# Loading a global filter's inputs in fp32 on one queue, with conversions on GpSimd, VectorE and ScalarE

## The chip, the cores and the metric

The kernel runs on one core of one Trainium2 chip. The metric is device time in microseconds for one launch; several runs are taken and their median is given. A profile of one execution comes with each kernel. The engines are named as the profile does: PE (TensorE matmul), PEld (its weight loads), DVE (VectorE), ACT (ScalarE), POOL (GpSimd) and SP (SyncE, which here only issues transfers; SPq is its instruction queue).

## The reference

Eight batches of 3,200 positions with 256 channels. A circular convolution along the sequence with a learned filter per channel, done in the frequency domain, and then a gated layer: a causal depthwise convolution of five taps gives a gate, which multiplies a projection, and a second projection follows. Inputs and output are fp32.

```python
X = np.fft.rfft(x, axis=1)                      # x: (8, 3200, 256)
Y = X * (filt_r + 1j * filt_i)[None]            # filt: (1601, 256)
x = np.fft.irfft(Y, n=3200, axis=1)
gate_pre = sum(conv_w[k] * xp[:, k:k + S, :] for k in range(5))   # causal, xp is x with 4 zeros ahead
gate = 1 / (1 + np.exp(-gate_pre))
out = (gate * (x @ w_val)) @ w_out
```

## The kernel before

The transform of length 3,200 = 128 x 25 is done in two stages of matmuls with tables of sines and cosines that the kernel makes itself at the start. For each batch the work is cut into seven chunks (NCH), and seven helper functions each do one stage of one chunk:

- `s1`: 128-point transform of a chunk of `xt` with the table `cf_t` into PSUM, DVE copies it to bf16 (`so`), SP stores it to a scratch tensor in DRAM (`dscr`).
- `load_t`: loads `tt` back from `dscr` in another layout, so that the 25-point transforms lie along the partitions. This relayout needs all seven stores of the batch.
- `s2`: the 25-point transforms (tables `wc_t`, `ws_t`, `wsn_t`), ACT copies PSUM to `xs`, and DVE multiplies by the filter in three operations, `za`, `zb` and `z` (with `fr_t`, `fm_t`, which hold the filter).
- `inva`: the inverse 25-point transforms (`vc_t`, `vs_t`, `vsn_t`), ACT copies to `u`, SP stores to a second scratch tensor, `escr`.
- `load_v`: loads `vt` back from `escr` in the first layout; again all of a batch's stores must have landed.
- `invb`: the inverse 128-point transform (`ci_t`), which leaves the result `yt` channel-major; ACT copies it.
- `conv`, `val`, `outp`: the five taps as diagonal matmuls (`dg_t`) with a sigmoid on ACT (`gt`); the projection, multiplied on DVE (`gv`); the output projection, copied to `o` by DVE or ACT in turn and stored by SP.

A loop over sub-steps G starts, in each, one chunk of each stage, with a lag between stages: `s2` runs 9 sub-steps after `s1`, `inva` 10, `invb` 19, `conv` 21, `val` 22, `outp` 23. All seven `load_t` of a batch are called at once after its last `s1`, and all seven `load_v` after its last `inva`. Four PSUM tiles are shared by all stages in turn, so that a stage's matmuls wait until the tile of an earlier stage has been copied out.

The order on each engine is made by the framework's scheduler from the program's order and its estimates; the helpers' order in the loop is a preference, not a rule. Each engine executes its own list in order. SP carries all transfers but three kinds: x (line 86), the filter (lines 216 to 225) and the two projection weights are issued by POOL, in a form of transfer that converts fp32 to bf16 on the way. Ten `xt` buffers hold x, so POOL issues a load as soon as an `s1` has freed one.

Before the loop the tables are made: DVE reduces angles with `floormod` (seven operations, lines 103 to 113), ACT takes sines, and `expand` (line 171) spreads each table in thirteen small operations. The `s1` of batch 0 belongs to the loop's first sub-steps.

Of the kernel before, what the change touches and what calls it, by code (L numbers as in the profile page):

```python
# [15 lines left out]
PI = math.pi  # L16
# [19 lines left out]
def kernel(  # L36
# [31 lines left out]
    b_npi = cpool.tile([128, 1], FP32, name="b_npi")  # L68
# [3 lines left out]
    xpool = ctx.enter_context(tc.tile_pool(name="xin", bufs=10))  # L72
    spool = ctx.enter_context(tc.tile_pool(name="s1o", bufs=4))
    tpool = ctx.enter_context(tc.tile_pool(name="s2i", bufs=8))

    def psum():
        return pp.tile([128, 1024], FP32, name="ps", tag="ps")

# [3 lines left out]
    def load_x(b, j):  # L82
        p0, np_ = PCH[j]
        xt = xpool.tile([128, 4, D], BF16, name="xt")
        src = x[b].rearrange("(a r) d -> a r d", r=R)[:, p0:p0 + np_, :]
        nc.gpsimd.dma_start(out=xt[:, 0:np_, :], in_=src)  # L86
        xts[(b, j)] = xt

    for j in range(NCH):
        load_x(0, j)  # L90


    with tc.tile_pool(name="gen", bufs=1) as g1, \
         tc.tile_pool(name="gen2", bufs=2) as g2, \
         tc.tile_pool(name="genf", bufs=1) as gf:

        def floormod(src_ap, divisor):
            shp = list(src_ap.shape)
            divi = g2.tile(shp, I32, name=f"fm_i{shp[1]}")
            bak = g2.tile(shp, FP32, name=f"fm_b{shp[1]}")  # L100
            q = g2.tile(shp, FP32, name=f"fm_q{shp[1]}")
            cm = g2.tile(shp, FP32, name=f"fm_c{shp[1]}")
            nc.vector.tensor_scalar(divi[...], src_ap, 1.0 / float(divisor), None,
                                    op0=ALU.mult)
            nc.vector.tensor_copy(bak[...], divi[...])
            nc.vector.scalar_tensor_tensor(q[...], bak[...], -float(divisor), src_ap,
                                           op0=ALU.mult, op1=ALU.add)
            nc.vector.tensor_scalar(cm[...], q[...], float(divisor) - 0.5, None,
                                    op0=ALU.is_ge)
            nc.vector.scalar_tensor_tensor(q[...], cm[...], -float(divisor), q[...],  # L110
                                           op0=ALU.mult, op1=ALU.add)
            nc.vector.tensor_scalar(cm[...], q[...], -0.5, None, op0=ALU.is_lt)
            nc.vector.scalar_tensor_tensor(q[...], cm[...], float(divisor), q[...],
                                           op0=ALU.mult, op1=ALU.add)
            return q

        def iota(shape, pattern, base, cm, name):
            t = g1.tile(shape, FP32, name=name)
            nc.gpsimd.iota(t[...], pattern=pattern, base=base, channel_multiplier=cm,
                           allow_small_or_imprecise_dtypes=True)  # L120
            return t

        nc.vector.memset(b_npi[:, :], -PI)
        pcol = iota([128, 1], [[0, 1]], 0, 1, "pcol")


        kc = iota([128, NG, 2, GL], [[5, NG], [0, 2], [1, GL]], 1, 0, "kc")
        nc.vector.memset(kc[:, NG - 1, 0, GL - 1:GL], 0.0)
        pr = g1.tile([128, NG, 2, GL], FP32, name="pr")
        nc.vector.tensor_scalar(pr[...], kc[...], pcol[:, 0:1], None, op0=ALU.mult)  # L130
        nc.vector.tensor_scalar(pr[:, :, 0, :], pr[:, :, 0, :], 0.75 * L, None,
                                op0=ALU.add)
        q = floormod(pr[...].rearrange("p g c l -> p (g c l)"), L)
        nc.scalar.activation(cf_t[:, :], q[...], AF.Sin, bias=b_npi[:, 0:1],
                             scale=2.0 * PI / L)

        ident = g1.tile([128, 128], FP32, name="ident")
        nc.vector.memset(ident[:, :], 1.0)
        nc.gpsimd.affine_select(out=ident[:, :], in_=ident[:, :], pattern=[[1, 128]],
                                compare_op=ALU.is_equal, fill=0.0, base=0,  # L140
                                channel_multiplier=-1)
        idh = g1.tile([128, 128], FP16, name="idh")
        nc.vector.tensor_copy(idh[:, :], ident[:, :])


        rq = floormod(pcol[...], R)
        lp = g1.tile([128, 1], FP32, name="lp")
        nc.vector.tensor_tensor(lp[...], pcol[...], rq[...], op=ALU.subtract)
        nc.vector.tensor_scalar(lp[...], lp[...], 1.0 / R, None, op0=ALU.mult)
        rp = g1.tile([128, 1], FP32, name="rp")  # L150
        nc.vector.tensor_copy(rp[...], rq[...])
        lw = g1.tile([128, 1], FP32, name="lw")
        nc.vector.tensor_scalar(lw[...], pcol[...], 4.0 * R - 0.5, None, op0=ALU.is_ge)
        nc.vector.tensor_scalar(lw[...], lw[...], -65.0, None, op0=ALU.mult)


        mk = g1.tile([128, GL, R], FP16, name="mk")
        mkf = g1.tile([128, GL, R], FP32, name="mkf")
        nc.vector.memset(mkf[...], 1.0)
        nc.gpsimd.affine_select(out=mkf[...], in_=mkf[...], pattern=[[-R, GL], [0, R]],  # L160
                                compare_op=ALU.is_ge, fill=0.0, base=0,
                                channel_multiplier=1)
        nc.gpsimd.affine_select(out=mkf[...], in_=mkf[...], pattern=[[R, GL], [0, R]],
                                compare_op=ALU.is_ge, fill=0.0, base=R - 1,
                                channel_multiplier=-1)
        nc.vector.tensor_copy(mk[...], mkf[...])

        def expand(dst, src):
            nc.gpsimd.memset(dst[:, :, P2:128], 0.0)
            for g in range(NG):  # L170
                nc.vector.tensor_tensor(
                    dst[:, g, 0:P2].rearrange("p (l r) -> p l r", l=GL),
                    src[:, g, :].unsqueeze(1).to_broadcast((128, GL, R)),
                    mk[...], op=ALU.mult)

        def negate(dst, src):
            nc.vector.tensor_scalar(dst[...], src[...], -1.0, None, op0=ALU.mult)

        def sincos(prod, dc, ds, dsn):
            qs = floormod(prod[...].rearrange("p g r -> p (g r)"), N)  # L180
            sn = g2.tile([128, NG, R], FP16, name="sn")
            nc.scalar.activation(sn[...].rearrange("p g r -> p (g r)"), qs[...],
                                 AF.Sin, bias=b_npi[:, 0:1], scale=2.0 * PI / N)
            pc = g2.tile([128, NG, R], FP32, name="pc")
            nc.vector.tensor_scalar(pc[...], prod[...], 0.75 * N, None, op0=ALU.add)
            qc = floormod(pc[...].rearrange("p g r -> p (g r)"), N)
            cs = g2.tile([128, NG, R], FP16, name="cs")
            nc.scalar.activation(cs[...].rearrange("p g r -> p (g r)"), qc[...],
                                 AF.Sin, bias=b_npi[:, 0:1], scale=2.0 * PI / N)
            expand(dc, cs)  # L190
            expand(dsn, sn)
            negate(ds, dsn)

        HK = R // 2 + 1
        kv = g1.tile([128, NG, R], FP32, name="kv")
        nc.gpsimd.iota(kv[:, :, 0:HK], pattern=[[5, NG], [L, HK]], base=1,
                       channel_multiplier=0, allow_small_or_imprecise_dtypes=True)
        nc.gpsimd.iota(kv[:, :, HK:R], pattern=[[5, NG], [-L, R - HK]],
                       base=1 + L * (R - 1), channel_multiplier=0,
                       allow_small_or_imprecise_dtypes=True)  # L200
        nc.vector.tensor_scalar(kv[...], kv[...], lp[:, 0:1], None, op0=ALU.add)
        nc.vector.tensor_scalar(kv[:, NG - 1, :], kv[:, NG - 1, :], lw[:, 0:1], None,
                                op0=ALU.add)
        nc.vector.tensor_scalar(kv[...], kv[...], rp[:, 0:1], None, op0=ALU.mult)
        sincos(kv, wc_t, ws_t, wsn_t)


        fi_t = gf.tile([128, NG, D], BF16, name="fi_t")

        def fsrc(f, row, ap):  # L210
            return bass.AP(tensor=f.tensor, offset=f.offset + row * D, ap=ap + [[1, D]])

        for f, dst in ((filt_r, fr_t), (filt_i, fi_t)):
            for l in range(GL):
                ng = NG if l < GL - 1 else NG - 1
# [187 lines left out]
    def invb(b, j):  # L403
# [15 lines left out]
        if j == 0:  # L419
            nc.gpsimd.memset(y[:, :, 0:H, 0:1], 0.0)  # L420
            for dh in range(2):
                nc.gpsimd.tensor_copy(y[:, dh, 0:H, 1:L], y[:, dh, R:R + H, 0:L - 1])
# [68 lines left out]
    for G in range(total):  # L491
        c = at(G, -NCH)
        if c is not None:
            load_x(*c)
# [57 lines left out]
```

## Time and profile before

| | us |
|---|---|
| median of 3 runs (lowest, highest) | 386.45 (383.33, 387.43) |
| profiled execution | 387.95 |
| its span | 385.9 |
| PE busy, share | 312.3, 81% |
| DVE busy, share | 284.9, 74% |
| ACT busy, share | 229.1, 59% |
| POOL busy, share | 64.2, 17% |

The profile counts the time from the first to the last instruction as the span; the launch lies around it. Matmuls are pipelined and their ends are modelled, so a PE that is shown busy can still be waiting a little. The transfers moved 94.5 MB: 79.0 MB on the queue that SP feeds and 15.0 MB on the one that POOL feeds, counted in the bytes that are written. The mean clock of TensorE was 0.966 of full speed.

### The profile page before, as it was taken

The numbers are of one execution on the slowest core, as the hardware profiler recorded it, in microseconds if no ns is written. First come the engines' busy times: TensorE is split into PE (matmuls) and PEld (weight loads), VectorE is DVE, ScalarE is ACT, GpSimd is POOL, SyncE is SP. The second block draws the span as 40 slices with busy tenths as digits, with TensorE's granted clock in tenths as the row PEclk, the third lists the DMA queues.
The fourth block names the chain that finished last, engine by engine and source line by source line (L and its number), as shares of the span: only waits on it lengthen the run. The fifth ranks groups of instructions, "written<-read, shape, count | busy, mean of one in ns | idle before, by whom it ended". The sixth has DMA issues, their size and how long they took to land.

```text
span 385.9 us, 8019 instructions
## 1 busy us (share of the span) xinstructions
PE 312.3 (81%) x3089; PEld 206.9 (54%) x3089; DVE 284.9 (74%) x462; ACT 229.1 (59%) x255; POOL 64.2 (17%) x131
## 2 busy tenths in 40 slices
PE   0230477475899999999997999899999999999992
PEld 0100145253656756766675666566676677666661
DVE  4999958553858887888787789678977677765554
ACT  1100235334976777677765776677677878867660
POOL 8797211112110211021102011100010001001000
PEclk9999998766989999999999999999999999999998
DMA  7999999999999999999999999989595968449343
GB/s 124 144 162 190 216 257 251 231 250 280 179 250 249 311 286 273 263 282 332 274 301 303 286 269 298 285 299 319 201 351 170 304 223 299 136 142 323 141 191 152
DMA packets 94118, 94.53 MB, mean 245 GB/s; under 512 B 10102, under 2 KB 74624, under 8 KB 94080
## 3 DMA queue, kind: packets, MB, share of 16 engines
q1 hardware_dynamic: 80064, 78.98, 62.5%
q0 software_dynamic: 14016, 15.04, 28.1%
q8 instruction: 24, 0.39, 0.4%
q14 instruction: 14, 0.11, 0.1%
HBM read 56.59 MB, written 52.43 MB: 282 GB/s over the span
## 4 chain that ended last, share of the span: by engine, by line
PE 44%; DVE 20%; DMA 19%; SPq 8%; issue 4%; ACT 2%; POOL 1%; DVEq 0%; ACTq 0%; POOLq 0%
PE ps L431 12%; PE ps L448 7%; DMA escr<-u 6%; PE ps L465 6%; DVE so L310 6%; DMA vt<-escr 5%; SPq L326 5%; PE ps L413 5%; DMA dscr<-so 4%; PE ps L376 3%; DVE gv L453 3%; DMA tt<-dscr 3%; PE ps L378 3%; PE ps L307 3%; DVE za L354 2%
## 5 line engine op out<-in xcount | busy, mean ns | idle before, releaser
L415 ACT ACTIVATE yt<-ps 128x1024 bf16<-128x1024 f32 (+1 forms) x56 | 52.1, 931 | 44.3 <-PE ps L413 44.2
L453 DVE TENSOR_TENSOR gv<-ps,gt 128x1024 bf16<-128x1024 f32 (+1 forms) x56 | 61.9, 1104 | 18.7 <-PE ps L448 13.7
L310 DVE CAST so<-ps 128x1024 bf16<-128x1024 f32 (+1 forms) x56 | 61.5, 1103 | 19.0 <-PE ps L307 15.9
L354 DVE TENSOR_TENSOR za<-xs,fr_t 125x1024 bf16<-125x1024 bf16 (+1 forms) x56 | 37.3, 665 | 50.5 <-ACT xs L349 50.3
L381 ACT ACTIVATE u<-ps 125x1024 bf16<-125x1024 f32 (+1 forms) x56 | 53.9, 963 | 24.4 <-PE ps L378 21.6
L431 PE MATMUL ps<-yt,dg_t 64*64 64x512 bf16 (+1 forms) x1120 | 65.7, 361 | 0.8
L349 ACT ACTIVATE xs<-ps 125x1024 bf16<-125x1024 f32 (+1 forms) x56 | 54.0, 965 | 19.6 <-PE ps L346 18.4
L436 ACT ACTIVATE gt<-ps 128x1024 bf16<-128x1024 f32 (+1 forms) x56 | 52.4, 935 | 9.1 <-PE ps L431 5.9
L86 POOL DMA_DIRECT2D xt<-in_x_dram x56 | 30.2, 569 | 153.0 <-PE ps L307 146.5
L307 PE MATMUL ps<-xt,cf_t 128*128 128x512 bf16 x112 | 36.9, 421 | 22.4 <-DVE so L310 11.4
L465 PE MATMUL ps<-wo_t,gv 128*128 128x256 bf16 x400 | 52.8, 273 | 0.9 <-DVE gv L453 0.9
L448 PE MATMUL ps<-yt,wv_t 128*128 128x512 bf16 (+1 forms) x224 | 52.6, 357 | 0.0
L465 PEld LDWEIGHTS <-gv 128*128 128x128 bf16 x400 | 39.1, 98 | 14.9 <-DVE gv L453 1.2
L413 PE MATMUL ps<-ci_t,vt 128*128 128x128 f16 x400 | 31.9, 221 | 13.3 <-DMA vt<-escr 9.6
L431 PEld LDWEIGHTS <-dg_t 64*64 64x64 bf16 x1120 | 30.1, 106 | 23.2 <-issue 10.1
L340 PE MATMUL ps<-tt,wc_t 125*128 125x256 bf16 x104 | 30.1, 289 | 12.9 <-DMA tt<-dscr 10.6
L470 DVE COPY o<-ps 128x1024 f32<-128x1024 f32 (+1 forms) x32 | 36.7, 1148 | 1.1 <-PE ps L465 1.1
L360 DVE TENSOR_TENSOR z<-za,zb 125x1024 bf16<-125x1024 bf16 (+1 forms) x56 | 36.4, 650 | 1.3
L413 PEld LDWEIGHTS <-vt 128*128 128x128 bf16 x400 | 27.0, 98 | 17.9 <-DMA vt<-escr 10.7
L358 DVE TENSOR_TENSOR zb<-xs,fm_t 125x1024 bf16<-125x1024 bf16 (+1 forms) x56 | 36.2, 646 | 0.0
L376 PE MATMUL ps<-z,vc_t 125*128 125x256 bf16 x104 | 30.0, 289 | 6.9 <-DVE z L360 6.9
L307 PEld LDWEIGHTS <-cf_t 128*128 128x128 f16 x112 | 9.2, 108 | 41.7 <-issue 28.2
(109 smaller groups left out, 386.6 us busy)
## 6 DMA issues: line engine op xcount, KB each, us to landing
out_dram<-o SPq DMA_DIRECT2D x32, 512.0 KB
tt<-dscr SPq DMA_DIRECT2D x48, 256.0 KB
escr<-u SPq DMA_DIRECT2D x48, 224.0 KB
out_dram<-o SPq DMA_DIRECT2D x24, 384.0 KB
xt<-in_x_dram POOLq DMA_DIRECT2D x32, 256.0 KB, 6.5
dscr<-so SPq DMA_DIRECT2D x32, 256.0 KB
vt<-escr SPq DMA_DIRECT2D x32, 256.0 KB
xt<-in_x_dram POOLq DMA_DIRECT2D x24, 192.0 KB, 5.7
```

The lines of the kernel that those rows point to most:

```text
L307: nc.tensor.matmul(ps[:, a * D:e * D], lhsT=cf_t[:, 0:128], rhs=xt[:, a:e, :], start=True, stop=True)
L310: nc.vector.tensor_copy(so[:, 0:np_, :].rearrange("p a d -> p (a d)"), ps[:, 0:np_ * D])
L349: nc.scalar.activation(xs[0:P2, 0:ng, :, :].rearrange("p g c d -> p (g c d)"), ps[0:P2, 0:ng * 512], AF.Copy)
L354: nc.vector.tensor_tensor(za[0:P2, 0:ng], xs[0:P2, 0:ng], fr_t[0:P2, g0:g0 + ng, :].unsqueeze(2).to_broadcast((P2, ng, 2, D)), op=ALU.mult)
L381: nc.scalar.activation(u[0:P2, 0:2 * ng, :].rearrange("p q d -> p (q d)"), ps[0:P2, 0:ng * 512], AF.Copy)
L413: nc.tensor.matmul(ps[:, o:o + L], lhsT=v[:, a, 128 * dh:128 * dh + 128], rhs=ci_t[:, :], start=True, stop=True)
L415: nc.scalar.activation(y[:, :, H + p0:H + p0 + np_, :].rearrange("p h a n -> p h (a n)"), ps[:, :].rearrange("p (h n) -> p h n", h=2)[:, : ...
L431: nc.tensor.matmul(ps[64 * dh:64 * dh + 64, 512 * r:512 * r + np_ * L], lhsT=dg_t[rows, dh, k, :], rhs=y[rows, dh, p0 + k:p0 + k + np_, :] ...
L436: nc.scalar.activation(g[:, :, 0:np_ * L], ps[:, :].rearrange("p (h n) -> p h n", h=2)[:, :, 0:np_ * L], AF.Sigmoid)
L448: nc.tensor.matmul(ps[:, 512 * eh:512 * eh + np_ * L], lhsT=wv_t[:, dh, 128 * eh:128 * eh + 128], rhs=y[:, dh, H + p0:H + p0 + np_, :], st ...
L453: nc.vector.tensor_tensor(gv[:, :, 0:np_ * L], ps[:, :].rearrange("p (h n) -> p h n", h=2)[:, :, 0:np_ * L], g[:, :, 0:np_ * L], op=ALU.mult)
L465: nc.tensor.matmul(ps[:, D * a:D * a + D], lhsT=gv[:, eh, L * a:L * a + L], rhs=wo_t[:, eh, :], start=(eh == 0), stop=(eh == 1))
```

## The change

- x is loaded in fp32 by SP into six new buffers (`xf`), and POOL converts each chunk to bf16 (`cast_x`) into four `xt` buffers; before, POOL issued converting loads into ten.
- The filter is loaded in fp32 by SP, in pieces between the stores of batch 0's `s1`; DVE converts the real part (`fr_t`), ACT scales and converts the imaginary part (`fm_t`), which DVE did before.
- SP's list is exactly the program's order (`manual_schedule`). A sub-step's order is `invb`, `s2`, `conv`, `cast_x`, `s1`, `inva`, `load_x`, `load_t`, `load_v`, `val`, `outp`, with one `load_t` and one `load_v` in each sub-step. The loads of `tt` of batch 0 and of x of batch 1 alternate before the loop.
- Lags: `s2` 10, `inva` 11, `invb` 21, `conv` 23, `val` 24, `outp` 25. `s1` of batch 0 stands before the making of the other tables, and ACT copies its chunks 1, 3 and 5.
- Angles are reduced by adding and subtracting a large constant (three operations), `expand` is one operation per table, negation and `dg_t` go from DVE to ACT, and the shift of `yt` by one (before two operations on POOL) is one on DVE.
- Buffers: `za` and `zb` two instead of three, `o` three instead of four.

```diff
-    xpool = ctx.enter_context(tc.tile_pool(name="xin", bufs=10))
+    xpool = ctx.enter_context(tc.tile_pool(name="xin", bufs=4))
+    fpool = ctx.enter_context(tc.tile_pool(name="xf", bufs=6))
...
+    ctx.enter_context(tc.manual_schedule(engines={E.SP}))
...
     def load_x(b, j):
         p0, np_ = PCH[j]
+        xf = fpool.tile([128, 4, D], FP32, name="xf")
+        src = x[b].rearrange("(a r) d -> a r d", r=R)[:, p0:p0 + np_, :]
+        nc.sync.dma_start(out=xf[:, 0:np_, :], in_=src)
+        xts[(b, j)] = xf
+
+    def cast_x(b, j):
+        np_ = PCH[j][1]
+        xf = xts[(b, j)]
         xt = xpool.tile([128, 4, D], BF16, name="xt")
-        src = x[b].rearrange("(a r) d -> a r d", r=R)[:, p0:p0 + np_, :]
-        nc.gpsimd.dma_start(out=xt[:, 0:np_, :], in_=src)
+        nc.gpsimd.tensor_copy(xt[:, 0:np_, :], xf[:, 0:np_, :])
         xts[(b, j)] = xt
...
+        if b == 0 and j % 2 == 1:
+            st[("Sact", j)] = nc.scalar.activation(sov, ps[:, 0:np_ * D], AF.Copy)
+        else:
+            nc.vector.tensor_copy(sov, ps[:, 0:np_ * D])
...
+        def sine(dst, t):
+            r = g2.tile(list(t.shape), FP32, name=f"sr{t.shape[1]}")
+            nc.vector.tensor_scalar(r[...], t, MAGIC, None, op0=ALU.add)
+            nc.vector.tensor_scalar(r[...], r[...], -MAGIC, None, op0=ALU.add)
+            nc.vector.tensor_tensor(r[...], t, r[...], op=ALU.subtract)
+            nc.scalar.activation(dst, r[...], AF.Sin, scale=2.0 * PI * (1.0 - 2e-7))
...
+        for j in range(NCH):
+            s1(0, j)
+            if 1 <= j <= GL:
+                load_f(j - 1)
...
-        def expand(dst, src):
+        def expand(eng, dst, src):
             nc.gpsimd.memset(dst[:, :, P2:128], 0.0)
-            for g in range(NG):
-                nc.vector.tensor_tensor(
-                    dst[:, g, 0:P2].rearrange("p (l r) -> p l r", l=GL),
-                    src[:, g, :].unsqueeze(1).to_broadcast((128, GL, R)),
-                    mk[...], op=ALU.mult)
+            return eng.tensor_tensor(
+                dst[:, :, 0:P2].rearrange("p g (l r) -> p g l r", l=GL),
+                src[...].unsqueeze(2).to_broadcast((128, NG, GL, R)),
+                mk[...].unsqueeze(1).to_broadcast((128, NG, GL, R)), op=ALU.mult)
...
+        for j in range(NCH):
+            load_t(0, j)
+            load_x(1, j)
...
+        with tc.issue_after(vs_ins.ins):
+            nc.vector.tensor_copy(fr_t[0:P2, :, :], ff[0:P2, 0])
+        nc.scalar.activation(fm_t[0:P2, :, 0, :], ff[0:P2, 1], AF.Copy,
+                             scale=sgn[0:P2, 0:1])
+        nc.scalar.activation(fm_t[0:P2, :, 1, :], ff[0:P2, 1], AF.Copy,
+                             scale=sg[0:P2, 0:1])
...
         if j == 0:
-            nc.gpsimd.memset(y[:, :, 0:H, 0:1], 0.0)
-            for dh in range(2):
-                nc.gpsimd.tensor_copy(y[:, dh, 0:H, 1:L], y[:, dh, R:R + H, 0:L - 1])
+            nc.vector.memset(y[:, :, 0:H, 0:1], 0.0)
+            nc.vector.tensor_copy(y[:, :, 0:H, 1:L], y[:, :, R:R + H, 0:L - 1])
...
-    LAG_S2 = 9
-    LAG_IB = LAG_S2 + 10
+    LAG_S2 = 10
+    LAG_IB = LAG_S2 + 11
...
+    steps = [
+        (invb, LAG_IB, 0), (s2, LAG_S2, 0), (conv, LAG_IB + 2, 0), (cast_x, -2, 1),
+        (s1, 0, 1), (inva, LAG_S2 + 1, 0), (load_x, -NCH, 2), (load_t, NCH, 1),
+        (load_v, LAG_S2 + 1 + NCH, 0), (val, LAG_IB + 3, 0), (outp, LAG_IB + 4, 0),
+    ]
     for G in range(total):
...
+        for stage, lag, first in steps:
+            c = at(G, lag, first)
+            if c is not None:
+                stage(*c)
```

`load_f(l)` issues four transfers (eight for the last l) of twelve or thirteen partitions each. `at(G, lag, first)` gives the batch and chunk that a stage handles in sub-step G, and nothing for batches below `first`.

## The prediction

> **What bounds the kernel now.** I read the time in stages first. The span is 385.9 us, the profiled run 387.95 us, so 2.05 us lie around the span; the median of the three runs, 386.45, is 0.4% below that run. Cut at the first stage-2 matmul (45.0 us), at the first `invb` (92.7) and at the 35th `invb` (280.1), the windows view answers (columns: stretch, its length, busy us of PE, PEld, DVE, ACT and POOL with counts, TensorE clock, DMA share, GB/s):
>
> ```profile
> 0.00:45.00 45.00, 8.33 (x19) 2.13 (x19) 38.35 (x157) 3.96 (x6) 34.13 (x70) 1.00 1.09 164
> 45.00:92.70 47.70, 29.52 (x165) 19.21 (x166) 30.76 (x43) 18.29 (x19) 5.59 (x12) 0.83 1.05 244
> 92.70:280.10 187.40, 176.20 (x1797) 119.74 (x1798) 147.10 (x184) 133.93 (x147) 20.68 (x41) 0.98 0.98 278
> 280.10:385.90 105.80, 98.26 (x1112) 65.87 (x1109) 68.64 (x80) 72.96 (x83) 3.75 (x8) 0.99 0.65 221
> ```
>
> PE is idle in 37 of the first 45 us and 18 of the next 48; then it is busy to 94%. The front is therefore latency, the rest a tight pipeline. Next, SP's timeline shows why the front drags: six relayout loads of batch 0 hold SP for 17 us, and everything else of SP stands behind them.
>
> ```profile
> 34.18 17.15 SPq L326 DMA_DIRECT2D tt<-dscr  x6
> ```
>
> Third, the chain of waits inside one sub-step of the middle (start us, us, what):
>
> ```profile
> 177.70 0.62 PE ps L413 x8
> ...
> 178.34 0.89 ACT yt L415
> ...
> 179.28 1.03 ACT xs L349
> ...
> 180.33 0.69 DVE za L354
> 181.02 0.61 DVE zb L358
> ...
> 181.66 0.04 DVE z L360
> 181.70 0.57 issue
> 182.27 1.22 DVE so L310
> ```
>
> From `invb` to the next `invb` at 183.54 is 5.84 us, and DVE's za, zb, z and so are 3.2 of them. So DVE's order is on the path although DVE is busy in only 147.10/187.40 = 78%. Fourth, the waits (us, times, longest):
>
> ```profile
> DVE za L354 <- ACT xs L349: 50.3, 39, 2.6
> PEld L413 <- DMA vt<-escr: 10.7, 4, 5.0
> SPq L398 <- DMA escr<-u: 13.5, 8, 3.7
> ```
>
> The vt loads are all issued at the end of a batch's `inva` and come late: the sub-steps at 199.7 and 240.2 took 7.6 and 6.9 us where 5.0 to 5.9 is usual.
>
> **The change, part by part (b is the batch).**
>
> *Front, tables and batch 0.* DVE's seven-operation floormod (0.24 to 0.41 us each at 325 columns) becomes three operations, thirteen expands of 0.14 us become one of about 1 us (1,625 elements at the 0.58 ns each of L232's 1.93 us for 3,328). The first so moves from 22.87 to about 12 us: it now waits for the kv tables, which POOL makes after four casts. The 20 dg_t and the negations go to ACT, which was busy for 3.96 of 45 us; ACT's so of j=1,3,5 cost 1.0 us each there and unload DVE. But SP now issues 31 transfers (7 dscr, 24 filter pieces) before the first tt, and in its instruction list each waits for the one eight earlier. Filter pieces landed after 3.7 to 6.2 us in before; at 4.5 us, 31/8 x 4.5 = 17.5 us from so(0) at 13.4: the last dscr is issued at about 31 (before: 30.9), landed at 35 (3.1 to 5.6 us in the chain). PE's order then wants three s1 of batch 1 before the first s2 (before: two), so x(1,2) must land behind three tt: 2.3 MB at 250 to 350 GB/s, 7 to 9 us, then cast and s1, 2 us. First s2: **45 us, no gain**; bounds 41 (filter pieces at 3.7 us) to 52 (at 6.2).
>
> *45 us to the first `invb`.* Eleven sub-steps instead of ten (LAG_S2 + 11). Before they took 4.76 us each, with the tt arriving 5 us apart. Now the tt lie between x loads and are there by about 50 us. Work per sub-step: DVE 1.15 (so) + 3 x 0.65 = 3.1 us; transfers 0.5 MB (x) + 0.23 + 0.23 and later the loads, 12.3 MB in all at 352 GB/s = 3.2 us. I take 3.8, between that floor and 4.76: **42 us** (35 to 52) for 47.6.
>
> *The middle, 34 sub-steps on both sides.* With load_t and load_v one per sub-step and one sub-step more of slack, the vt waits (8.0 - 5.4, 7.6 - 5.4, 6.9 - 5.4 and 0.7 us) should go. What is late next: DVE's chain, or bytes. A batch moved 292 GB/s x 39.9 us = 11.65 MB; x in fp32 adds 1.64, so 13.3 MB. The best ten microseconds without any x load are
>
> ```profile
> 280.00:290.00 10.00, 9.88 (x113) 7.32 (x111) 8.06 (x11) 7.88 (x9) 1.16 (x2) 1.00 1.01 352
> ```
>
> and at 352 GB/s 13.3 MB need 37.8 us a batch, 5.39 a sub-step (before 5.61). Four sub-steps of ramp at 18 us and 30 x 5.39 = 162: **180 us** for 187.4 (bounds: 174, from PE alone, whose sub-steps without s1 between 306.2 and 334.8 us take 4.77 us, plus 0.43 for s1; and 187).
>
> *End.* The two more sub-steps of lag mean that at the 35th `invb` two s1, one s2 and one `inva` less are left, 2 x 0.43 + 2 x 0.85 = 2.6 us of a PE that is 93% busy: **103 us** for 105.8. The smaller pools (za, zb 2, o 3) cost nothing as long as each buffer is read within its sub-step.
>
> *yt's shift on DVE:* 1,016 elements a batch, 0.6 us at L232's pace, 1.2 at so's; DVE waits 50 us for xs in all, which hides it; uncovered 5 to 10 us.
>
> *The casts on POOL* are the unknown. L422's two copies took 1.16 us for 1,016 elements, so 1.17 us for 1,024 and 0.88 for 768: 7.3 us a batch on an engine that does little else. What they do to DVE can be bounded from one place:
>
> ```profile
> 209.07 1.16 POOL L422 COPY yt<-yt 128x508 bf16<-128x508 bf16 x2 [5.81 <-ACT yt L415]
> ```
>
> ```profile
> 209.96 0.82 DVE L354 TENSOR_TENSOR za<-xs,fr_t 125x1024 bf16<-125x1024 bf16 x1 [2.63 <-ACT xs L349]
> 210.70 0.68 DVE L358 TENSOR_TENSOR zb<-xs,fm_t 125x1024 bf16<-125x1024 bf16 x1
> ```
>
> za overlaps the copy for 0.27 us and takes 0.82 instead of 0.69; the same in five of five batches. gv at 351.86, under a copy for 0.5 us, takes its usual 0.96. So only za, zb and z suffer, by 0 (a cast beside so, gv, o) to 1.17 us (the whole cast). A cast can start when s1 has freed its xt; today's x loads have that trigger and fall at 192.35 (zb runs, z next) and 197.54 (zb runs, so next). In five of the seven sub-steps of DVE's new order z comes before so, in two the cast would run beside so for nothing. I take the low end, 0.1 us a sub-step or **3 us** in all, since DVE's next operation starts before the last has ended (0.61 apart at 0.69 us), which leaves a waiting cast no gap until so.
>
> [...]
>
> **Sum:** 45 + 42 + 180 + 103 + 3 = 373 us of span for 385.9; 375 with what lies around it; 374 against the median.
>
> **Rivals.**
> 1. *Half the cast's length reaches the chain* (za's 0.13 for 0.27 us of overlap): 0.5 us in five of seven of 41 sub-steps, 15 us: 373 - 3 + 15, about 385 us. For: the only overlap in the trace has that ratio. Against: it may be a start-up effect.
> 2. *Slower: casts hold off DVE for their whole length.* Place: between za, zb and z; price 1.05 us (mean) in the sub-steps whose chain runs through DVE, four of seven, so 4.4 us a batch with the rest: 22 us in the middle, 4.5 between 45 us and the first `invb`: 370 + 26 = 396, about 397 us. It decides as soon as a cast costs more than about 0.6 us in those sub-steps. For: za's stretch, and that s1 ends 0.3 to 0.9 us after za starts. Against: gv, so, o are free of it, and DVE idles 1.2 us before each za.
> 3. *Nothing is gained:* the transfers, at a share of 0.98 to 1.05 until 280 us, were the bound, or eight transfers in flight on one queue are too few; every stage keeps its length: 386 to 389 us. For: the share. Against: x loads wait for buffers (146.5 us on `PE ps L307`), not for DMA, and the share reached 1.01 without them.
> 4. *The change does not shift what it says:* the front's loads are no earlier since the queue order is fixed; that is already in the 45 us.
>
> **How the numbers follow.** This kernel's runs spread over 1.1%, so 1% is about what can be told from no change. Forecast 374: 0.45, own range 365 to 382. Rival 1, 385: 0.17. Rival 2, 397 (390 to 405): 0.30. Rival 3: 0.08. The range 365 to 401 leaves out the upper half of rival 2's tail and the forecast's lowest end. Faster: the forecast and a little of rival 1, 0.47; same 0.15; slower 0.38.
>
> **What would show it.** First s2 near 45 us and first `invb` near 87; sub-steps of 5.2 to 5.5 us with no 7 us outlier; vt no longer in PE's waits; POOL's casts at 1.1 to 1.2 us; za, zb, z still at a mean of 0.69. I am wrong if these rise to 0.9 or more, if the casts are much longer than L422's pace, or if SP shows waits on its own transfers of several us per sub-step.

## The result, and the profile after

The changed kernel takes **403.4 us** (median of 4 runs, 402.4 to 403.7), the kernel before 385.1 in the runs beside it: a ratio of **1.047** (95% interval 1.040 to 1.054), slower. Its profiled execution took 403.68 us with a span of 402.0, the one of before 387.95 and 385.9. Cut at the same events as before (first stage-2 matmul, first and 35th `invb`), the windows view of the kernel after gives (stretch, length, busy us of PE, PEld, DVE, ACT and POOL, TensorE clock, DMA share, GB/s):

```profile
0.00:58.10 58.10, 9.40 (x22) 2.76 (x23) 24.94 (x63) 19.95 (x33) 19.11 (x38) 1.00 0.86 208
58.10:104.80 46.70, 29.71 (x184) 19.62 (x183) 36.51 (x46) 20.34 (x21) 15.29 (x15) 0.85 0.93 298
104.80:299.40 194.60, 174.70 (x1797) 117.83 (x1798) 164.84 (x193) 134.81 (x147) 37.20 (x31) 0.99 0.96 309
299.40:402.00 102.60, 95.75 (x1092) 64.04 (x1089) 65.98 (x81) 71.18 (x81) 0.00 (x0) 0.99 0.69 226
```

Two stretches grew: the one before the first s2, from 45.0 to 58.1 us, and the middle, from 187.4 to 194.6. In the middle PE works no more than before (174.7 us), while DVE's busy time rises from 147.1 to 164.8. Little of that is more work (the shift of `yt`, one copy of 0.41 us a batch, is new on DVE; e5 below does the same work in 148.6 us); most of it is slower instructions.

SP's timeline shows what lengthened the front (start us, us, instruction):

```profile
28.04 0.35 SPq L134 DMA_DIRECT2D dscr<-so  x1
...
34.80 0.35 SPq L134 DMA_DIRECT2D dscr<-so  x1
...
43.11 0.35 SPq L134 DMA_DIRECT2D dscr<-so  x1
46.45 0.39 SPq L148 DMA_DIRECT2D tt<-dscr  x1
```

The last rows of batch 0 were ready at 28.4 us, but their store leaves at 43.1: the filter pieces stand between the stores, and the 24 pieces take from 14.1 to 42.4 us to issue, 1.2 us each, since in SP's list a piece waits for the transfer eight earlier (the store that left at 17.08 us lands at 25.14 and the piece eight places behind it leaves at 25.16; from 13 to 46 us SP's waits for filter pieces sum to 15.9 us). The relayout, and with it PE, starts after that.

For the middle, the page's groups show it (busy us, mean ns of one, idle before it), first before:

```profile
L354 DVE TENSOR_TENSOR za<-xs,fr_t 125x1024 bf16<-125x1024 bf16 (+1 forms) x56 | 37.3, 665 | 50.5 <-ACT xs L349 50.3
...
L360 DVE TENSOR_TENSOR z<-za,zb 125x1024 bf16<-125x1024 bf16 (+1 forms) x56 | 36.4, 650 | 1.3
...
L358 DVE TENSOR_TENSOR zb<-xs,fm_t 125x1024 bf16<-125x1024 bf16 (+1 forms) x56 | 36.2, 646 | 0.0
```

and after:

```profile
L98 POOL CAST xt<-xf 128x1024 bf16<-128x1024 f32 (+1 forms) x56 | 62.2, 1113 | 209.5 <-PE ps L126 124.3
...
L378 DVE TENSOR_TENSOR za<-xs,fr_t 125x1024 bf16<-125x1024 bf16 (+1 forms) x56 | 37.8, 676 | 39.5 <-ACT xs L373 39.5
...
L384 DVE TENSOR_TENSOR z<-za,zb 125x1024 bf16<-125x1024 bf16 (+1 forms) x56 | 50.0, 892 | 1.4
...
L382 DVE TENSOR_TENSOR zb<-xs,fm_t 125x1024 bf16<-125x1024 bf16 (+1 forms) x56 | 42.6, 762 | 0.0
```

Before, the three DVE products took 665, 646 and 650 ns; now za is the same, zb is 18% and z 37% longer. One place of POOL's timeline, and of DVE's at the same moment, shows how:

```profile
185.22 0.93 POOL L98 CAST xt<-xf 128x768 bf16<-128x768 f32 x1 [4.09 <-PE ps L126]
```

```profile
184.78 0.69 DVE L378 TENSOR_TENSOR za<-xs,fr_t 125x1024 bf16<-125x1024 bf16 x1 [0.26 <-ACT xs L373]
185.39 1.31 DVE L382 TENSOR_TENSOR zb<-xs,fm_t 125x1024 bf16<-125x1024 bf16 x1
186.73 0.69 DVE L384 TENSOR_TENSOR z<-za,zb 125x1024 bf16<-125x1024 bf16 x1
187.34 1.22 DVE L133 CAST so<-ps 128x1024 bf16<-128x1024 f32 x1
```

The cast starts when s1 has freed its buffer, while za still runs and just ahead of zb, and ends at 186.15. zb ends 0.55 us later, as if it had started only then; z, with no cast beside it, takes 0.69 again. A later cast starts when zb is already running:

```profile
203.62 1.58 POOL L98 CAST xt<-xf 128x1024 bf16<-128x1024 f32 x1 [4.71 <-DMA tt<-dscr]
```

```profile
203.62 0.68 DVE L382 TENSOR_TENSOR zb<-xs,fm_t 125x1024 bf16<-125x1024 bf16 x1
204.34 1.41 DVE L384 TENSOR_TENSOR z<-za,zb 125x1024 bf16<-125x1024 bf16 x1
```

zb keeps its 0.68, the cast takes 1.58 us where one that nothing holds takes 1.04 (e5's mean for this size), and z, the next product, again ends 0.55 us after the cast. So in these places a cast waited for the product that was running, and then got in ahead of the next one. The rest of the execution reads the same: all 27 full-size products that took over 0.75 us ended 0.54 or 0.55 us after the end of a cast.

Last, the waits of the whole execution (us, times, longest):

```profile
DVE za L378 <- ACT xs L373: 39.5, 38, 2.7
ACT fm_t L333 <- DMA ff<-in_filt_i_dram: 17.4, 1, 17.4
...
PE ps L437 <- DVE so L133: 12.8, 21, 1.3
...
PEld L437 <- DMA vt<-escr: 4.5, 3, 2.1
```

PE's wait for vt did shrink, as forecast (10.7 us on PEld before). In its place PE waits for DVE's so, which frees the PSUM tile and stands behind zb and z, 12.8 us where the kernel before had 3.7:

```profile
PE ps L413 <- DVE so L310: 3.7, 9, 0.7
```

`fm_t` shows the whole front in one line: ACT stands for 17.4 us until the last filter piece has landed.

### The profile page after: what moved, and what is told of

It reads as the page before. It is cut to its first block, busy times and chain, and to the rows that moved or that the text cites. A ratio compares the mean times of both kernels' runs of the same rounds, so it can differ in the third digit from the quotient of the medians.

```text
span 402.0 us, 8038 instructions
## 1 busy us (share of the span) xinstructions
PE 309.6 (77%) x3089; PEld 204.3 (51%) x3089; DVE 292.3 (73%) x381; ACT 246.3 (61%) x282; POOL 71.6 (18%) x83
## 4 chain that ended last, share of the span: by engine, by line
PE 45%; DMA 24%; DVE 18%; issue 4%; SPq 4%; ACT 3%; POOL 1%; DVEq 0%; ACTq 0%; POOLq 0%
PE ps L454 10%; DVE so L133 7%; PE ps L488 7%; PE ps L471 7%; DMA dscr<-so 5%; PE ps L437 4%; DMA xf<-in_x_dram 4%; DMA vt<-escr 4%; PE ps L400 4%; DVE zb L382 3%; PE ps L402 3%; DMA escr<-u 3%; PE ps L126 3%; DMA ff<-in_filt_i_dram 3%; DMA tt<-dscr 2%
## 5 line engine op out<-in xcount | busy, mean ns | idle before, releaser
L98 POOL CAST xt<-xf 128x1024 bf16<-128x1024 f32 (+1 forms) x56 | 62.2, 1113 | 209.5 <-PE ps L126 124.3
L439 ACT ACTIVATE yt<-ps 128x1024 bf16<-128x1024 f32 (+1 forms) x56 | 52.1, 931 | 45.7 <-PE ps L437 45.6
L476 DVE TENSOR_TENSOR gv<-ps,gt 128x1024 bf16<-128x1024 f32 (+1 forms) x56 | 61.7, 1101 | 19.3 <-PE ps L471 15.7
L133 DVE CAST so<-ps 128x1024 bf16<-128x1024 f32 (+1 forms) x53 | 58.5, 1104 | 11.4 <-PE ps L126 10.8
L378 DVE TENSOR_TENSOR za<-xs,fr_t 125x1024 bf16<-125x1024 bf16 (+1 forms) x56 | 37.8, 676 | 39.5 <-ACT xs L373 39.5
L384 DVE TENSOR_TENSOR z<-za,zb 125x1024 bf16<-125x1024 bf16 (+1 forms) x56 | 50.0, 892 | 1.4
L437 PE MATMUL ps<-ci_t,vt 128*128 128x128 f16 x400 | 31.6, 219 | 19.2 <-DVE so L133 12.8
L382 DVE TENSOR_TENSOR zb<-xs,fm_t 125x1024 bf16<-125x1024 bf16 (+1 forms) x56 | 42.6, 762 | 0.0
L437 PEld LDWEIGHTS <-vt 128*128 128x128 bf16 x400 | 26.8, 98 | 25.2 <-issue 19.7
```

What stands on the lines that cost most here:

```text
L98: nc.gpsimd.tensor_copy(xt[:, 0:np_, :], xf[:, 0:np_, :])
L133: nc.vector.tensor_copy(sov, ps[:, 0:np_ * D])
L382: nc.vector.tensor_tensor(zb[0:P2, 0:ng], xs[0:P2, 0:ng, ::-1, :], fm_t[0:P2, g0:g0 + ng], op=ALU.mult)
L437: nc.tensor.matmul(ps[:, o:o + L], lhsT=v[:, a, 128 * dh:128 * dh + 128], rhs=ci_t[:, :], start=True, stop=True)
L476: nc.vector.tensor_tensor(gv[:, :, 0:np_ * L], ps[:, :].rearrange("p (h n) -> p h n", h=2)[:, :, 0:np_ * L], g[:, :, 0:np_ * L], op=ALU.mult)
```

## The experiments

Two theories stood after the result. F: the front is late because of the filter pieces in SP's queue. C: the middle is longer because casts hold DVE's two-operand products off. Each had the rival that something else sets its stretch and that what is seen only fills idle time. In the expectations a "table store" is a store of `so` to `dscr`, and the "spread" of the tables is the loading of `tt` from it.

All stages in us; the stretches end at the first s2, the first and the 35th `invb`, and the end of the span. The ratio is against the kernel before on the same chip.

| kernel | median | ratio (95%) | to first s2 | to first `invb` | middle | rest |
|---|---|---|---|---|---|---|
| before | 385.1 | 1 | 45.0 | 47.7 | 187.4 | 105.8 |
| after | 403.4 | 1.047 (1.040, 1.054) | 58.1 | 46.7 | 194.6 | 102.6 |
| e1_filter_pool | 386.5 | 1.003 (0.999, 1.007) | 44.2 | 44.3 | 196.6 | 102.1 |
| e2_cast_gate | 399.2 | 1.035 (1.018, 1.052) | 58.0 | 44.5 | 193.7 | 102.6 |
| e3_x_pool | 392.9 | 1.019 (0.998, 1.039) | 58.3 | 41.1 | 187.3 | 102.2 |
| e4_memset | 395.0 | 1.024 (1.004, 1.044) | 58.6 | 44.4 | 189.5 | 103.0 |
| e5_filter_pool_gate | 378.3 | 0.980 (0.974, 0.986) | 44.9 | 40.0 | 188.4 | 102.2 |
| e6_filter_x_pool | 378.2 | 0.979 (0.972, 0.986) | 35.8 | 49.4 | 189.3 | 102.7 |
| e7_no_later_x | 370.1 | 0.965 (0.952, 0.978) | 46.0 | 38.5 | 182.6 | 101.9 |
| e8_lag_more | 380.9 | 0.990 (0.985, 0.995) | 45.5 | 43.8 | 189.6 | 99.5 |
| e9_filter_late | 417.7 | one run | 48.1 | 70.8 | 194.5 | 102.6 |
| e10_filter_spread | 401.4 | 1.043 (1.033, 1.054) | 56.5 | 44.8 | 194.9 | 102.6 |
| e11_filter_rows | 400.8 | 1.042 (1.028, 1.056) | 57.1 | 46.5 | 194.7 | 102.6 |
| e12_filter_wide | 406.4 | 1.052 (1.041, 1.062) | 61.7 | 45.7 | 194.0 | 102.5 |
| e13_filter_112 | 392.6 | 1.025 (1.021, 1.030) | 47.6 | 46.9 | 194.0 | 102.3 |

### The filter back on GpSimd (e1)

```diff
-            for c, f in ((0, filt_r), (1, filt_i)):
-                dst = ff[:, c]
-                nc.sync.dma_start(
+            for dst, f in ((fr_t, filt_r), (fi_t, filt_i)):
+                nc.gpsimd.dma_start(
```

> The kernel after, with its filter loads alone put back as before: GpSimd issues the 24 pieces, converting on the way, right after the rotary sines, and SP carries none of them; the fp32 tiles and DVE's and ScalarE's reads of them are gone. Theory F (in the kernel after, the last table store stood 14.7 us behind its rows in SP's queue, behind filter pieces that wait for the piece eight earlier, and with it the spread of the tables and the x loads): the last table store is issued at 29 to 31 us, the first x tile's spread by 34, the first s2 starts at 43 to 46 instead of 58.1, and the whole takes 387 to 391 us instead of 403.4, with the middle (first to 35th invb) unchanged at 193 to 196. Rival (the front is bound by what all loads together move, or by the tables on the other engines): the first s2 stays at 56 to 59 and the time at 401 to 404.

Measured: 386.5 us, half a microsecond under the range, and SP's timeline has the seven stores in one run, done by 22.0 us and not at 29 to 31:

```profile
13.27 8.76 SPq L134 DMA_DIRECT2D dscr<-so  x7
27.54 0.37 SPq L148 DMA_DIRECT2D tt<-dscr  x1
```

The relayout starts at 27.5 instead of 46.5, the first s2 at 44.2. Theory F holds, and moving the filter's loads is worth 16.9 of the 18.3 us lost. The edit changes their queue, the bytes that they write (half, since they convert) and their place in the program at once; e9 to e13 take these apart. The middle, 196.6, is no shorter than after.

### The casts (e2, e3, e4)

e2 lets a cast start only after z:

```diff
+            g = nc.gpsimd.tensor_copy(zt[0:P2, :], z[0:P2, 0, 0, 0:1])
+            with tc.issue_after(g.ins):
+                nc.gpsimd.tensor_copy(xt[:, 0:np_, :], xf[:, 0:np_, :])
```

> The kernel after, with one instruction added in front of each GpSimd cast of x from the first s2 on: a copy on GpSimd of one column of the sub-step's z, so that the cast cannot start until DVE has finished za, zb and z, and runs beside the table, gv and output work instead. Nothing else moves. Theory C (a cast and DVE's two-operand instructions hold each other off while both read SBUF, and this costs the 7 us by which the middle grew): za, zb and z come back from 676, 762 and 892 ns to 650 to 720 each, DVE's busy time for a batch falls from 36 to 32 to 34 us, a batch from 41.4 to 38 to 39.5, the first-to-35th invb from 194.6 to 178 to 186, and the whole to 384 to 395. Rival (the middle is set by SP's one queue or the transfers, and the longer z are filled idle time): za, zb and z shorten as well, but the batch stays at 41 to 41.5 and the time at 401 to 404.

The products are back at once, as the groups of e2 show:

```profile
L393 DVE TENSOR_TENSOR z<-za,zb 125x1024 bf16<-125x1024 bf16 (+1 forms) x56 | 37.5, 670 | 3.5
L387 DVE TENSOR_TENSOR za<-xs,fr_t 125x1024 bf16<-125x1024 bf16 (+1 forms) x56 | 37.2, 664 | 51.7 <-ACT xs L382 51.7
L391 DVE TENSOR_TENSOR zb<-xs,fm_t 125x1024 bf16<-125x1024 bf16 (+1 forms) x56 | 36.2, 646 | 0.0
```

So a cast beside so costs DVE nothing: at 189.29 us so takes its usual 1.22 with a whole cast of 0.83 beside it. The means of so, gv and o are 1,107, 1,104 and 1,147 ns, where the kernel before has 1,103, 1,104 and 1,148; beside POOL's copy of `yt` in that kernel o took 1.22 us (129.01) and gv 0.96 (351.86), as without it. A cast that got in ahead of zb or z cost most of its length: 0.63 us for one of 0.93 (185.39 us above), 0.72 where one that nothing holds takes 1.04 (204.34). But the middle is 193.7 us, hardly shorter, and the time 399.2: worse than theory C asked for, a little better than the rival (two runs, 397.8 and 400.5). PE's waits in the middle of e2 tell where the gain went:

```profile
PE ps L447 <- DMA vt<-escr: 13.7, 9, 2.4
PE ps L447 <- DVE so L142: 3.7, 6, 0.8
```

The wait for so fell by 8.9 us against the kernel after (12.6 in its middle), and the wait for vt rose by 9.1 (from 4.6). One limit had covered another.

> The kernel after, with x alone loaded as before: GpSimd issues converting transfers straight into ten bf16 tiles, there is no fp32 x tile and no cast, and everything else (filters in fp32 on SP, the order of SP's queue, the relayouts spread over the sub-steps) stays. Theory C (casts against DVE): za, zb and z at 650 to 700 ns, first to 35th invb 178 to 186 us, the first s2 earlier by 3 to 8 us since x need not wait its turn in SP's queue and there is no cast before s1, the whole 380 to 392. Rival (the middle is bound by the order of SP's one queue, relayouts above all): first to 35th invb stays at 192 to 195, and only the front changes: 395 to 401.

e3 has no cast at all, and its products take 651, 646 and 651 ns. Its middle is 187.3 us, that of before, outside what either theory gave: without casts the change's new order of SP's queue gains nothing there and loses nothing. The first s2 stays at 58.3, so it is the filter alone that delays it, not x.

> The kernel after, with the casts of x of the batches after the first replaced by a copy of one column and a GpSimd memset of the rest of the bf16 tile: GpSimd is busy at the same place for a similar time but reads no SBUF for it. It leaves out the conversion of x for every batch but the first. Theory C1 (what holds DVE off is that GpSimd reads SBUF beside DVE's two-operand reads): za, zb and z at 650 to 710 ns, first to 35th invb 178 to 186 us, the whole 385 to 394. Rival C2 (any GpSimd instruction of that length, writes too, holds DVE off): z stays at 800 ns or more and the time at 398 to 404.

```diff
+            g = nc.gpsimd.tensor_copy(xt[:, 0:np_, 0:1], xf[:, 0:np_, 0:1])
+            with tc.issue_after(g.ins):
+                nc.gpsimd.memset(xt[:, 0:np_, 1:D], 0.0)
```

Here POOL writes as much and reads next to nothing. POOL's timeline and DVE's at the same moment:

```profile
187.40 0.64 POOL L101 CAST xt<-xf 128x3 bf16<-128x3 f32 x1 [5.15 <-DMA tt<-dscr]
187.97 0.73 POOL L103 MEMSET xt<- 128x765 bf16 x1
```

```profile
187.30 0.68 DVE L387 TENSOR_TENSOR zb<-xs,fm_t 125x1024 bf16<-125x1024 bf16 x1
188.01 0.69 DVE L389 TENSOR_TENSOR z<-za,zb 125x1024 bf16<-125x1024 bf16 x1
```

z runs beside a memset of its own length and takes its usual 0.69. The copy of three elements a partition, which reads, took 0.64 us beside zb, where one of four elements took 0.20 at 192.81: it looks held off by zb in its turn. With the read gone and the write kept, DVE is free, so the read is the cause. Theory C1 holds for the mechanism (means 652, 646, 651 ns); the time, 395.0, is 1 us outside its range, because the middle, 189.5, stops short of 186.

### The two repairs together (e5, e6)

> The kernel after with its filter pieces issued by GpSimd, converting, as in e1_filter_pool, and each cast held back until the sub-step's z as in e2_cast_gate. If the two losses are separate and add up: 403.4 less 16.9 (e1) less 4.2 (e2), so 380 to 385, with the first s2 at 43 to 46, first to 35th invb at 190 to 195 and PE waiting 7 to 10 us for vt in those. If an earlier start makes the middle's transfers collide more: 385 to 390.

> The kernel after with x and the filters both loaded as before, converting by GpSimd, and no cast: what is left of the change is the order of SP's queue, the table store and relayouts spread over the sub-steps and the later lags. If the losses add up: first s2 at 43 to 46 (e1), ramp 41 and middle 187 (e3), end 102, so a span of 373 to 378 and 375 to 380 in all, 1 to 2.5% faster than before. If x, back on GpSimd's queue, delays the filters there or the front's transfers collide: first s2 at 50 or later and 383 or more.

Both take 378.2 to 378.3 us, 2% less than the kernel before and 6% less than the kernel after. On top of e1 the gate is worth 8.3 us by the medians (11.7 between the two profiled spans, 8.2 of them in the middle); on the kernel after alone it was worth 4.2. The two repairs together bring more than the sum of each alone, 25.2 us against 21.1. Part of it is that TensorE's granted clock was 0.96 in one batch of e2's profile, where PE's busy time is 38.1 us instead of 36.7; why e2 waited so much longer for vt is not settled. e6 reached its time by another way than expected: the first s2 at 35.8 instead of 43 to 46, then 49.4 us to the first `invb`, where the filter, now issued behind x on POOL, is late in its turn: ACT's second `fm_t` ends only at 48.3 us, and the first zb waits for it.

### What holds the middle at 188 us (e7, e8)

Without the casts' harm, the middle is 187 to 190 us in five kernels (before, e3, e4, e5, e6; e2, with 193.7, is the exception), not the 180 of the prediction.

> e5_filter_pool_gate, without the loads of x for the third batch and later: their casts read one tile loaded for the second batch (left out: the x of batches 2 to 7, some 3.3 MB a batch of the transfers). In e5 and every other kernel here the DMA engines show a busy share of 0.97 to 1.03 through the middle, and a batch takes 39.5 to 41 us with PE busy 37; in the last batch, where no x is loaded, the share is 0.9 and the batch takes 38.6. If what the transfers take together holds the middle: batches of 37.5 to 38.3 us, PE's waits for vt nearly gone, first to 35th invb 180 to 184 instead of 188.4, the whole 369 to 373. If it is the chain of instructions (casts, so, the relayout's own latency): 187 to 189 and 376 to 379.

```diff
+        if b >= 2:
+            xts[(b, j)] = last_x[0]
+            return
```

> e5_filter_pool_gate with one more sub-step between the relayout and invb (the lag from s2 to invb 12 instead of 11), so that each vt load has a sub-step of some 5.5 us more to land. If vt is late for its latency alone: PE's waits for vt, 6.6 us of the middle in e5, go, first to 35th invb 181 to 184, and with one more sub-step before the first invb the whole stays at 375 to 378. If the transfers are the limit, the same waits turn up elsewhere: 186 to 189 and 378 to 383.

The middles of e5 and of e7 in the windows view:

```profile
84.90:273.30 188.40, 172.08 (x1768) 116.66 (x1797) 148.57 (x194) 133.94 (x147) 36.46 (x68) 0.99 0.98 319
```

```profile
84.50:267.10 182.60, 172.01 (x1796) 116.98 (x1797) 150.22 (x196) 134.15 (x148) 36.58 (x68) 1.00 0.80 254
```

With x's transfers gone the DMA share drops to 0.80 and 5.8 us go; PE's wait for vt falls from 8.7 us to 1.9. The batches take an even 38.8 to 39.1 us, a little over the 37.5 to 38.3 expected. Not all of the 5.8 us belongs to the transfers: 2.4 of them fall in the first batch, where TensorE's granted clock was 0.95 in e5 and 1.00 in e7 (PE busy 30.8 and 29.5 us). At a clock of 1.00 in both, the second batch takes 38.8 us in either, and the third and fourth are 1.7 and 1.8 us shorter in e7. With more lag instead (e8) the wait for vt goes as well, but another transfer is late in its place, and the middle is 189.6 (some 2 us of it from one batch with a granted clock of 0.96):

```profile
PE ps L371 <- DMA tt<-dscr: 7.5, 7, 1.6
PE ps L445 <- DVE so L142: 6.4, 12, 0.8
```

So it is not one relayout's latency that makes these loads late, it is what the DMA engines carry in all, and that is worth some 4 to 6 us of the middle. The 182.6 us that are left without x's loads, 38.8 a batch with PE busy for 37, no run here takes apart. That x stands in SP's queue isn't it either: e3 and e6 load it from POOL's queue and keep 187 to 189 us at a share of 0.97 to 0.98.

### Why the filter pieces are slow (e9 to e13)

> The kernel after, filters still in fp32 on SP, but their pieces issued after the spread of the tables and between the x loads of the second batch, so that no table store stands behind a piece. If SP's order alone made the first s2 late: the last table store at 28 to 31 us, first s2 at 43 to 48, but the filters land 10 us or more later than in the kernel after, the first z waits for fr_t until 55 to 62, and what was won before s2 is lost before the first invb: 398 to 406 in all. If the pieces are slow wherever they stand and take the table's bandwidth: first s2 at 50 or later.

```diff
         for j in range(NCH):
             s1(0, j)
-            if 1 <= j <= GL:
-                load_f(j - 1)
...
             load_t(0, j)
             load_x(1, j)
+            if 1 <= j <= GL:
+                load_f(j - 1)
```

First s2 at 48.1, as order alone would have it, but the pieces, with loads of x and `tt` between them, now take from 25.6 to 70.3 us, the first zb waits until 78.7, and the whole is 417.7 us, not the 398 to 406 expected. The pieces are slow wherever they stand. The next four runs ask why.

> The kernel after with the same 24 fp32 filter pieces on SP in another order: one piece writes 12 or 13 partitions, and in the kernel after eight pieces in flight write 50 of them (two of the five groups of 25); here consecutive pieces go to all five groups in turn. If the pieces are slow (1.2 us apart, 83 ns for a packet of 1 KB) because those in flight crowd on few partitions: pieces 0.6 to 0.8 us apart, the last table store at 29 to 35 instead of 43.1, first s2 at 45 to 50, the whole 389 to 396. If the place they write to does not matter (the source, 1 KB rows far apart, or the packets themselves): first s2 at 56 to 59, 401 to 405.

```diff
+        for c, f in ((0, filt_r), (1, filt_i)):
+            for half in range(2):
+                for l in (0, 3, 1, 4, 2):
+                    pieces.append((c, f, half, l))
```

> The kernel after with each of the 20 large filter pieces reading as many rows, but consecutive ones: each partition takes 13 rows that follow one another in DRAM instead of 13 rows five apart, and the next partition goes on where this one ends, not 128 rows away. The pieces, their sizes, their places in SP's queue and the partitions they write are the same (left out: the right filter rows, so the output is that of another filter). If the scattered source makes the pieces slow: 0.6 us or less apart, first s2 at 44 to 48, the whole 387 to 393. If it is the partitions they write to or eight in flight: first s2 at 55 to 59 and 400 to 405.

```diff
-                    in_=fsrc(f, l + 1, [[L * D, HK], [GL * D, ng]]))
+                    in_=fsrc(f, 300 * l, [[ng * D, HK], [D, ng]]))
```

Neither moved much: last table store at 42.5 and 41.4 instead of 43.1, times 401.4 and 400.8. The second says that the scattered source is not the cause; the first rules out the order of the pieces.

> The kernel after with the same fp32 bytes for the filter on SP, cut the other way: 26 pieces of 125 KB, each writing one row of 1 KB to all 125 partitions, from 125 consecutive rows, instead of 24 pieces that write up to 13 rows to 12 or 13 partitions (left out: the right filter rows, so the output is that of another filter). Neither the order of the pieces (e10) nor consecutive source rows (e11) made them faster. If a transfer to 12 or 13 partitions is slow by itself, since the engines work through one piece after the other: the pieces leave 0.5 us or less apart, the last table store at 28 to 32 instead of 43.1, first s2 at 44 to 48, the whole 387 to 393. If it is fp32 rows of 1 KB on this queue, or eight transfers in flight: 1.0 us apart or more, first s2 at 54 to 59, 399 to 405.

```diff
+            for c, f, g in pieces[5 * k:5 * k + (5 if k < GL - 1 else 6)]:
+                nc.sync.dma_start(out=ff[0:P2, c, g, :],
+                                  in_=fsrc(f, 120 * g, [[D, P2]]))
```

Wide pieces are no faster: 29.1 us for the 26, 1.1 us each, and 406.4 us in all. But the windows of the kernel after and of e12 differ in one column, the DMA share:

```profile
30.00:40.00 10.00, 0.00 (x0) 0.00 (x0) 0.00 (x0) 0.00 (x0) 0.00 (x0) 1.00 0.86 164
```

```profile
30.00:40.00 10.00, 0.00 (x0) 0.00 (x0) 0.00 (x0) 1.32 (x1) 0.00 (x0) 1.00 0.41 147
```

From 30 to 42 us the kernel after moved 1,981 packets, most of them of 1 KB, at a share of 0.86, which is 16 x 12 x 0.86 / 1,981 = 83 ns of an engine for each; e12 moved 1,631 at 0.401, 47 ns each. The packets got faster, but the engines stood idle for most of the time: outside short bursts, when a `dscr` store (128 partitions) is under way, the share is 0.3 to 0.4 (34 of the window's 40 slices). e13 therefore writes 112 partitions a piece (P2 is 125), the other 13 with two pieces at the end:

```diff
-                nc.sync.dma_start(out=ff[0:P2, c, g, :],
-                                  in_=fsrc(f, 120 * g, [[D, P2]]))
+                nc.sync.dma_start(out=ff[0:112, c, g, :],
+                                  in_=fsrc(f, 120 * g, [[D, 112]]))
```

> As e12_filter_wide (same fp32 bytes on SP, other rows of the filter, so that the output is that of another filter), but each of the 26 pieces writes 112 partitions, a multiple of 16, and two pieces at the end bring the remaining 13 partitions. In e12 a packet of 1 KB took 49 ns instead of 83, but the DMA engines' share fell to 0.33 to 0.41 at 120 GB/s, as if a third of the 16 engines carried the 125 rows. If the cut of a piece is what limits these loads: a share near 0.9 and 250 GB/s or more while they run, the pieces 0.35 to 0.5 us apart, the last table store at 27 to 33, first s2 at 43 to 49, the whole 386 to 394. If it is SP's queue or the fp32 rows: 1 us apart as before, first s2 at 55 to 62, 399 to 407.

```profile
20.00:30.00 10.00, 0.00 (x0) 0.00 (x0) 7.81 (x17) 6.37 (x13) 0.18 (x1) 1.00 1.00 285
```

```profile
25.81 0.37 SPq L134 DMA_DIRECT2D dscr<-so  x1
...
30.00 0.35 SPq L134 DMA_DIRECT2D dscr<-so  x1
36.08 0.39 SPq L148 DMA_DIRECT2D tt<-dscr  x1
```

The same bytes of fp32 filter, the same queue, the same stores between the pieces: now 285 GB/s, 15.9 us for the 28 pieces or 0.57 us each, the last store at 30.0 us, first s2 at 47.6, the whole 392.6. Since other source rows alone changed little (e11), that settles it: it was the cut of the pieces, and not the queue, the bytes or the fp32 rows. It cost 10.5 of the 13.1 us by which the first s2 missed its forecast.

## Why the prediction was wrong

It said 374 us and the time is 403.4, 2.4 us above the range. By its own sum, 373 us of span against 402.0:

- **45 us to the first s2: the first failed step, 13.1 us.** The order was read rightly: SP's list, eight transfers in flight, `dscr` stores behind pieces. The term that was mis-sized is "4.5 us for a filter piece with eight in flight", that is 0.56 us a piece. It was 1.18 us (28.3 us for 24), so some 9.4 us for eight, and the last `dscr` store left at 43.1 us where the forecast had about 31. The 3.7 to 6.2 us came from POOL's converting loads, which write half the bytes; another cut of the same bytes (e13) has 0.57 us a piece and the last store at 30.0, the forecast's own place. The upper bound, 52, took the slowest of those loads, and the pieces here were slower than that.
- **42 us to the first `invb`:** 46.7. Casts again: with the filter on POOL the stretch is 44.3 with casts that start at will (e1) and 40.0 with casts held back (e5).
- **180 us for the middle, plus 3 for the casts: the second failed step, 11.6 us.** Both terms were too small: without the casts' harm the middle is 188.4 us (e5), 8.4 over the 180, and the kernel after has 6.2 more, where 3 were allowed.
- *The casts* were taken at their low end, on the argument that DVE's operations leave a waiting cast no gap. A waiting cast does get in, ahead of the next product, and that product waits for all of it (203.62 us above). The place that the prediction quotes reads the same way: L422's copy ends at 210.23 us and za at 210.78, again 0.55 us later, so za had not been slowed at half rate, it had been held until the copy's end. That is rival 2's mechanism, "casts hold off DVE for their whole length", which had 0.30. In a full batch six of the seven sub-steps have a zb or z that is 0.5 to 0.85 us longer, 4.0 us in all, near that rival's 4.4. Over the execution zb and z lost some 20 us of DVE's time (50.0 + 42.6 us against 36.9 + 36.1 in e5), but the gate gains back 8.3 us of the whole and not 26; why the rest does not reach the time was not measured. The rival's time, 397, came near the result by luck: an unforeseen 13 us of the front made up for its high price.
- *The transfers.* "The vt waits should go" was half right: PEld's wait fell from 10.7 to 4.5 us, but once the casts are tamed the transfers are late again (e2, e5), and the middle is no shorter than before. The 180 was worked out from 13.3 MB a batch at 352 GB/s, read from a stretch without x loads. e5's two longest batches moved 330 and 327 GB/s at a share of 1.01 and 0.99; at that rate 13.3 MB need 40.3 to 40.7 us, and these batches took 40.5 and 40.9, not 37.8. Rival 3's argument, the DMA share of about 1, was given 0.08 and came nearer for the middle.
- **103 us for the end:** 102.6. Right, and so was the shorter table work: the first so is at 12.0 us, as forecast.

Of the signs of being wrong that the prediction named, two showed: z rose to 0.89 us, practically the 0.9 named (zb to 0.76, za hardly), and SP stood behind its own transfers, though in the front alone. The casts had nearly the forecast pace: 1.22 and 0.97 us by size for 1.17 and 0.88, and 1.04 and 0.84 where nothing held them (e5).

## What to carry to other kernels

When a queue carries loads behind which something urgent waits, work out their rate from the cut of the transfer and not only from its bytes: here 112 partitions a piece went nearly twice as fast as 125 or as 12 and 13 (15.9 us to issue them all, 29.1 and 28.3). Work put on GpSimd that reads SBUF was free beside so, gv and o (1.22, 0.96 and 1.22 us beside a cast or a copy, as without), which have one SBUF input or none, and not beside products with two (zb from 0.68 to 1.31 us, z from 0.69 to 1.41); place it there, with a data dependence if need be, or load with conversion and have none. And before a stall is written off as gain, ask which resource has a share near 1: in e2's middle the DMA share was 0.97, and while the waits for so fell by 8.9 us, those for vt rose by 9.1.

## What the runs showed of the hardware that was not expected

- The same 3,250 rows of 1 KB in 24 to 28 transfers on one queue took 28.3 us to issue with 12 or 13 partitions a piece, 29.1 with 125 and 15.9 with 112; what the core moved meanwhile, stores included, was about 164 GB/s, 120 to 147 and 285. With 125 partitions the DMA share was 0.3 to 0.4 between bursts, with 112 it was 1.0, and with 12 or 13 it was 0.87 from 41 to 43 us, with almost nothing but filter pieces in flight. Which engines carried a piece, and so why the share follows the cut, no run shows.
- A high share did not make the pieces of 12 or 13 partitions fast: from 30 to 40 us the core moved 164 GB/s at 0.86, where e13 moved 285 at 1.00 (20 to 30 us). A packet took 83 ns of an engine's time on average when pieces wrote 12 or 13 partitions and 47 ns when they wrote 125. In e10, whose neighbouring pieces write far apart, the loads were hardly faster (last table store at 42.5 us instead of 43.1), so what made these packets slow stays open.
- A GpSimd memset of 0.73 us beside z did not lengthen it (0.69 us), while a copy of 3 elements a partition was itself held from 0.20 to 0.64 us beside zb.
